# Zero products in TensorE's early waits and full-tile score biases for the first two head pairs, in a windowed-attention and gated token-mixing kernel on one core

## The chip, the core and the metric

The kernel runs on one core of a Trainium2 chip. The core has five engines that work side by side, each on its own list of instructions: TensorE (matrix products, written PE in the profile; PEld is its loading of weights), VectorE (DVE), ScalarE (ACT), GpSimd (POOL) and SyncE (SP). They wait for each other by semaphores. Products land in PSUM, everything else is in SBUF. The metric is the device time of one execution in microseconds; less is better. Three executions of the kernel before give a median of 172.1 us.

## What is computed

A windowed attention with a few global tokens, and a layer that mixes tokens and channels behind it. Inputs and output are float32; B = 4 batches, H = 8 heads, S = 768 tokens, D = 64, so d_model = 512; 8 global tokens, a window of 96.

```python
scores = scale * np.matmul(q, k.transpose(0, 1, 3, 2))
is_global = pos[None, :] < int(n_global)
is_local = (rel >= 0) & (rel < int(n_local))
dist = np.where(is_global & ~is_local, float(n_local), np.abs(rel))
scores = scores - slopes[:, None, None] * dist          # slope by head
scores = np.where(is_global | is_local, scores, -1e9)
a = softmax(scores);  x = (a @ v)  as [B, S, H * D]

theta = x @ w_theta
zr, zi = x * np.cos(theta), x * np.sin(theta)
y = einsum('ts,bsd->btd', w_tok_r, zr) + einsum('ts,bsd->btd', w_tok_i, zi)
u = x + y
out = u + np.maximum(u @ w_ch, 0.0)
```

## The kernel before

**Tiling.** Tokens lie in six tiles of 128. Heads go in four pairs p = 0 to 3, the two heads of a pair in the lower and upper 64 partitions of kT and qT (head dimension on the partitions, tokens along the row). Since a token sees at most the 95 before it and the 8 global ones, each key tile meets its own query tile and the next; kG holds the keys of a tile with those of the global tokens put in. The 11 blocks of a head are done in three chunks c = 0, 1, 2 (four, four and three blocks of 128 columns), so one chunk of a pair is a score tile pb of 128 x 2 x 512 in PSUM. Two such tiles exist (pool `big`); all smaller products take one of four rotating slots (pool `small`, tiles named ps).

**Batch 0** is written out by hand, in the order in which each engine runs it (lines 92 to 646): no scheduler moves anything there. Its exponentials are made by ScalarE from a score tile to which the bias has already been added in PSUM. For that `score_bias(p, c)` (L292) first writes `diag[h]` times `dist` into the tile, where `diag[h]` is the identity times -slope/scale and `dist` the table of distances (1e6 where nothing is seen); `score_mms` (L309, products at L325) then adds the keys times the queries on top, and `score_exp` (L331, L335) takes the exp. A score tile is free for the next bias when its exp has run.

`score_bias` has two forms. One makes two products of 128x128 weights, one for each head (L298). The other makes four of 64x64 weights (L305): since `diag` is diagonal, its two diagonal 64x64 quarters suffice, and for the second head of the pair rows and columns are swapped by halves, for which `distS` is `dist` with its halves of partitions swapped (`swap_distances`, L135, VectorE). Pair 0's chunks 0 and 1 take the first form, all others the second.

**The front of the program**, on TensorE: `warm(6)` makes six products of a tile of zeros into a slot of ps (L192, L195), the results of which nobody reads. Then come the biases of chunks (0,0) and (0,1), the transposes of pair 0's k and then q (`turn0`, L223, products at L221; they need the loaded and cast inputs), its scores for chunk 0 (`score_mms(0, 0, 0)`), which wait for the copies of the transposes to kT and qT (`out0`, L232) and to kG (`kglob`, L241 and L243) by ScalarE and VectorE. Then pair 1's transposes and the scores of chunk (0,1). The loop at L583 goes on over the pairs: exp of chunk (p,1), the copies of the next pair's kT, qT and kG, bias and scores of chunk (p,2), the products with the values of the pair before (`values`, L387), exp of (p,2), then bias, scores and exp of the next pair's chunk 0, bias and scores of its chunk 1, and the transposes of the pair after that. Behind it come theta (L428), the sines, the token mix (L453) and the channel product (L481), and the later batches, whose attention (with the bias as a factor after the exp) is woven between them.

## Time and profile before

| what | us |
|---|---|
| median of three runs | 172.1 (171.46, 172.1, 172.4) |
| the profiled execution, own time | 171.59 |
| its span, first to last instruction | 169.5 |
| TensorE busy | 157.9 (93% of the span) |
| VectorE busy | 126.7 (75%) |
| ScalarE busy | 104.6 (62%) |
| GpSimd busy | 38.9 (23%) |
| chain that ended last: TensorE's share | 62% |
| 64x64 bias products (L305), 40 of them, 394 to 400 ns each (median) | from 9.8 to 21.4 us |
| full bias products (L298), 4 of them, 634 ns each | from 3.7 to 5.0 us |
| products of the zero tile (L195), 6 of them, 634 ns each (median) | from 1.2 to 3.3 us |

Busy time counts a product from its start to its modelled end, and products overlap, so the duration of one is longer than the distance to the next. The span leaves out about 2.1 us around the first and last instruction. In the lists of instructions a row is: start, length, engine, line, operation, output <- inputs, shapes, and a count where equal instructions are merged; brackets hold the idle time before it on its engine and the instruction that ended this. In the chain of waits each row is one link, followed back from the end of the program.

### The profile page before, as it was taken

The numbers are of one execution on the slowest core, as the hardware profiler recorded it, in microseconds if no ns is written. First come the engines' busy times: TensorE is split into PE (matmuls) and PEld (weight loads), VectorE is DVE, ScalarE is ACT, GpSimd is POOL, SyncE is SP. The second block draws the span as 40 slices with busy tenths as digits, with TensorE's granted clock in tenths as the row PEclk, the third lists the DMA queues.
The fourth block names the chain that finished last, engine by engine and source line by source line (L and its number), as shares of the span: only waits on it lengthen the run. The fifth ranks groups of instructions, "written<-read, shape, count | busy, mean of one in ns | idle before, by whom it ended". The sixth has DMA issues, their size and how long they took to land.

```text
span 169.5 us, 3785 instructions
## 1 busy us (share of the span) xinstructions
PE 157.9 (93%) x1550; PEld 84.9 (50%) x1572; DVE 126.7 (75%) x265; ACT 104.6 (62%) x134; POOL 38.9 (23%) x46
## 2 busy tenths in 40 slices
PE   7579989999989999999989999999999999999991
PEld 2246665657655455545545464444555544444440
DVE  6848877699999997989998697787877837614442
ACT  4699898995599694799842641999257109400010
POOL 8975339005164101049700000000000000000000
PEclk9999999999999999999999999999999999999999
DMA  4999999999999999809999796777138472233335
GB/s 151 200 169 178 210 206 205 204 208 182 150 202 221 150 175 157 152 5 201 136 110 144 196 178 139 135 149 221 32 77 142 111 169 95 95 62 93 93 96 182
DMA packets 72704, 25.34 MB, mean 150 GB/s; under 512 B 60784, under 2 KB 69744, under 8 KB 72688
## 3 DMA queue, kind: packets, MB, share of 16 engines
q0 software_dynamic: 45696, 12.45, 88.6%
q1 hardware_dynamic: 26576, 12.13, 32.5%
q10 hardware_dynamic: 416, 0.52, 0.9%
q8 instruction: 12, 0.20, 0.6%
q14 instruction: 4, 0.03, 0.1%
HBM read 25.69 MB, written 6.29 MB: 189 GB/s over the span
## 4 chain that ended last, share of the span: by engine, by line
PE 62%; DVE 17%; ACT 13%; DMA 4%; issue 2%; DVEq 0%; SPq 0%
PE ps L453 27%; PE ps L481 9%; PE pb L428 6%; ACT e L335 5%; PE pb L325 5%; ACT cs L438 4%; PE pb L387 4%; PE ps L428 3%; DMA qk<-in_k_dram 3%; PE ps L267 2%; DVE x_sb L394 2%; DVE e L344 2%; DMA xT<-x_sb 2%; DVE kG L241 2%; PE ps L405 2%
## 5 line engine op out<-in xcount | busy, mean ns | idle before, releaser
L453 PE MATMUL ps<-zri,w_tokT 128*128 128x512 bf16 x272 | 67.8, 380 | 0.8 <-issue 0.2
L335 ACT ACTIVATE e<-pb 128x1024 bf16<-128x1024 f32 (+1 forms) x48 | 43.6, 955 | 16.7 <-PE pb L325 16.3
L453 PEld LDWEIGHTS <-w_tokT 128*128 128x128 bf16 x288 | 25.9, 98 | 27.3 <-DVE w_tokT L189 0.6
L458 DVE TENSOR_TENSOR u<-x_sb,ps 128x512 bf16<-128x512 bf16 x24 | 16.4, 684 | 13.3 <-PE ps L453 12.9
L481 PE MATMUL ps<-w_ch_bf,uT 128*128 128x512 bf16 (+1 forms) x96 | 23.9, 370 | 0.2
L442 DVE TENSOR_TENSOR zri<-x_sb,cs 128x1024 bf16<-128x1024 bf16 (+1 forms) x30 | 16.6, 581 | 5.0 <-ACT cs L438 4.7
L486 DVE SCALAR_TENSOR_TENSOR o_sb<-ps,u 128x512 f32<-128x512 f32 (+1 forms) x25 | 16.4, 664 | 4.4 <-PE ps L481 4.4
L325 PE MATMUL pb<-qT,kT 64*128 64x128 bf16 x224 | 15.4, 219 | 3.3 <-DVE qT L232 1.4
L344 DVE TENSOR_TENSOR e<-e,etab 128x1024 bf16<-128x1024 bf16 (+1 forms) x24 | 14.8, 620 | 2.3 <-ACT e L335 2.3
L325 PEld LDWEIGHTS <-kT 64*128 64x128 bf16 x224 | 8.8, 94 | 14.5 <-issue 10.5
L472 ACT COPY uT<-ps 128x512 bf16<-128x512 bf16 x7 | 4.2, 597 | 18.9 <-PE ps L471 18.8
L438 ACT ACTIVATE cs<-pb,halfpi 128x1024 bf16<-128x1024 f32 x8 | 8.9, 1115 | 10.7 <-PE pb L428 10.6
L428 PE MATMUL pb<-w_theta_bf,xT 128*128 128x512 bf16 x62 | 15.0, 379 | 0.2
L387 PEld LDWEIGHTS <-e 128*128 128x128 bf16 x352 | 12.7, 97 | 3.7 <-issue 1.2
L481 PEld LDWEIGHTS <-uT 128*128 128x128 bf16 x100 | 9.1, 98 | 9.9 <-ACT uT L472 0.8
L428 PEld LDWEIGHTS <-xT 128*128 128x128 bf16 x96 | 8.9, 98 | 10.1 <-DMA xT<-x_sb 0.6
L88 POOL DMA_DIRECT2D vn<-in_v_dram x5 | 9.6, 1916 | 11.4 <-DVE qkn L252 10.4
L325 PE MATMUL pb<-qT,kG 64*128 64x128 bf16 x128 | 11.8, 217 | 0.3 <-DVE kG L243 0.2
L394 DVE TENSOR_TENSOR x_sb<-pb,rec 128x768 bf16<-128x768 f32 x12 | 11.5, 958 | 0.4
L347 DVE TENSOR_TENSOR e<-e,etab 128x1024 bf16<-128x1024 bf16 x12 | 8.3, 689 | 2.9 <-ACT e L335 2.8
L387 PE MATMUL pb<-vn,e 128*128 128x65 bf16 x168 | 9.7, 193 | 0.3 <-DVE e L344 0.2
L273 ACT COPY kT<-ps 128x768 bf16<-128x768 bf16 x8 | 6.3, 800 | 5.2 <-PE ps L267 5.1
(81 smaller groups left out, 213.1 us busy)
## 6 DMA issues: line engine op xcount, KB each, us to landing
out_dram<-o_sb SPq DMA_DIRECT2D x23, 256.0 KB, 2.3
vn<-in_v_dram POOLq DMA_DIRECT2D x3, 768.0 KB, 23.1
qk<-in_q_dram POOLq DMA_DIRECT2D x2, 768.0 KB, 20.6
qk<-in_k_dram POOLq DMA_DIRECT2D x2, 768.0 KB, 22.2
w_nat<-in_moe_w_tok_r_dram POOLq DMA_DIRECT2D x3, 384.0 KB, 13.0
w_nat<-in_moe_w_tok_i_dram POOLq DMA_DIRECT2D x3, 384.0 KB, 14.1
vn<-in_v_dram POOLq DMA_DIRECT2D x2, 384.0 KB, 10.2
qk<-in_q_dram POOLq DMA_DIRECT2D x8, 96.0 KB, 10.1
```

The costliest lines, as they stand in the source:

```text
L325: nc.tensor.matmul(pb[:, hh, o:o + T], lhsT=lhsT, rhs=qT[R, (own, nxt)[part]], start=bool(b), stop=bool(b) or (jt == NT - 1 or (j == 1 and ...
L335: ins = nc.scalar.activation(e_c, pb[:, :, 0:n], AF.Exp, scale=scale).ins
L344: nc.vector.tensor_mul(e_c, e_c, tab[:, :, s0:s0 + n // T].rearrange("p a s n -> p a (s n)"))
L387: nc.tensor.matmul(po4[:, head - h0, it - i0], lhsT=l_, rhs=r_, start=(i_ == 0), stop=(i_ == len(mms) - 1))
L394: nc.vector.tensor_mul(xv, po4[:, :, :, 0:D], rec.to_broadcast([T, n, nt, D]))
L428: nc.tensor.matmul(pb[j_] if last else pb[:, j_, :], lhsT=xT[:, dc, st(j_)], rhs=w_theta_bf[:, dc, :], start=(dc == 0), stop=(dc == NC - 1))
L438: nc.scalar.activation(o, p_, AF.Sin, **bias)
L442: anchor["zri"] = nc.vector.tensor_mul(zri[b][:, i_, 2 * c + j_:2 * c + j_ + n, :].rearrange("p j (g d) -> p j g d", g=NP), xb[:, :, 2 * c ...
L453: anchor["pe"] = nc.tensor.matmul(ps, lhsT=w_tokT[wi][:, st, tt * T:(tt + 1) * T], rhs=zri[b][:, wi, st, :], start=(st == 0 and wi == 0), ...
L458: anchor["dve"] = nc.vector.tensor_add(u_sb[b, tt].rearrange("p (g d) -> p g d", g=NP), x_sb[b][:, :, tt, :], ps.rearrange("p (g d) -> p g ...
L481: nc.tensor.matmul(ps_c, lhsT=uT[:, dc, :], rhs=w_ch_bf[:, dc, i_ * n:(i_ + 1) * n], start=(dc == 0), stop=(dc == NC - 1))
L486: nc.vector.scalar_tensor_tensor(o_sb[:, cols], in0=ps_c, scalar=0.0, in1=u[:, cols], op0=ALU.max, op1=ALU.add)
```

## The change

Two things, in batch 0's hand-written part alone.

The full form of the bias is taken for all three chunks of pairs 0 and 1, so for (0,2), (1,0), (1,1) and (1,2) besides the two that had it. And `warm` is called three times more: with three products behind pair 0's second set of transposes, and with one product each before and after the bias of chunk (1,0).

```diff
         pb = pbs[0, p, c] = ps_big()
         n = min(4, 2 * NT - 1 - 4 * c)
         s0 = 2 if c else 0
-        if p == 0 and c < 2:
+        if p < 2:
             for hh in range(2):
                 nc.tensor.matmul(pb[:, hh, 0:n * T], lhsT=diag[:, 2 * p + hh],
                                  rhs=dist[:, s0:s0 + n].rearrange("p s n -> p (s n)"),
...
     turn0(0, 0)
+    warm(3)
     swap_distances()
     diagonals(1)
     out0(0, 1, act, 0)
...
         if p == 0:
             vglob(0, 0, 4)
+        if p == 0:
+            warm(1)
         score_bias(p + 1, 0)
+        if p == 0:
+            warm(1)
         score_mms(0, p + 1, 0)
         score_exp(0, p + 1, 0)
         score_bias(p + 1, 1)
```

## The prediction

> **What bounds the kernel now.** I read the page first: the span, the row of TensorE's busy tenths and the row of its granted clock.

> ```profile
> span 169.5 us, 3785 instructions
> ...
> PE   7579989999989999999989999999999999999991
> ...
> PEclk9999999999999999999999999999999999999999
> ```

> A slice is 4.24 us. From the fourth slice on TensorE is nearly always busy, so the tail is TensorE's, and what the front hands over late arrives late at the end. All edits lie in the first four slices. The PEclk row says full clock from the first slice. The durations by line say otherwise; the columns are the count and then minimum, median and maximum in ns, of products of one shape (128x512, bf16):

> ```profile
> L195 PE MATMUL ps<-zero x6: 608/634/634, 1.2 to 3.3; 128*128 128x512 bf16 x6
> ...
> L298 PE MATMUL pb<-dist,diag x4: 634/634/634, 3.7 to 5.0; 128*128 128x512 bf16 x4
> ...
> L453 PE MATMUL ps<-zri,w_tokT x272: 377/379/390, 31.4 to 162.4; 128*128 128x512 bf16 x136
> ```

> The same shape takes 634 ns up to 5.6 us and 379 ns later: TensorE starts slow, and the granted clock's row doesn't show it. When does it change? The transposes of L221 take 219 ns at 6.0 us and at 17.3 us alike, so in this execution TensorE is fast from 6.0 us on.

> Then TensorE's instructions in order of time: start, length, line, and in brackets the idle time before and what ended it.

> ```profile
> 3.73 1.91 PE L298 MATMUL pb<-dist,diag 128*128 128x512 bf16 x4
> 6.00 0.86 PE L221 MATMUL ps<-ident,qk 128*64 128x128 bf16 x24 [0.36 <-DVE qk L216]
> 8.31 0.34 PE L325 MATMUL pb<-qT,kT 64*128 64x128 bf16 x6 [1.44 <-DVE qT L232]
> ...
> 10.94 0.40 PE L305 MATMUL pb<-dist,diag 64*64 64x512 bf16 x2 [0.49 <-ACT e L335]
> ...
> 11.64 0.34 PE L325 MATMUL pb<-qT,kT 64*128 64x128 bf16 x6 [0.28 <-ACT kT L232]
> 12.18 0.23 PE L325 MATMUL pb<-qT,kG 64*128 64x128 bf16 x2 [0.20 <-DVE kG L243]
> ```

> Four waits: 1.44 us, ended by a VectorE copy of qT; 0.49 us, by the exp that frees a score tile; 0.28 us, by ScalarE's kT copy; 0.20 us, by VectorE's kG. Last the chain of waits (start, length, what), which says where TensorE itself is the limit:

> ```profile
> 8.31 0.40 PE pb L325 x8
> 8.71 0.79 PE ps L221 x24
> 9.50 0.35 PE pb L325 x8
> 9.87 1.02 ACT e L335
> ...
> 15.44 0.42 DVE kG L243
> ...
> 15.91 0.23 PE pb L325 x2
> 16.14 0.34 PE pb L305 x4
> 16.48 0.33 PE pb L325 x8
> ...
> 29.17 1.73 PE ps L428 x8
> ```

> From 8.31 to 9.87 us and from 15.91 to 17.6 us TensorE is on the chain. Between these the chain runs over ScalarE's exp and copies and VectorE's kG.

> **The change, part by part.** The instruction orders of VectorE, ScalarE, GpSimd and SyncE stay as they are, line for line, and no DMA moves. TensorE gets five products of the zero tile and loses eight: each of four bias chunks, (0,2), (1,0), (1,1), (1,2), is two full products instead of four of 64x64.

> *One product.* Eight 128x512 products in a row take 1.73 us (the last line above): 0.216 us each at the fast clock. The first six take 3.73 - 1.19 = 2.54 us: 0.42 us each at the slow one.

> *warm(3), after the second set of transposes.* These end issuing at 6.0 + 0.79 = 6.79 us; three products end by 7.44 us, at the slow clock by 8.06 us. The score products behind them wait for qT until 8.27 us. Cost 0; the cover is the wait of 1.44 us, and if that were gone the price would be 0.65 us.

> *A bias chunk.* From the four 64x64 products to the next line it is 0.34 us for 512 columns (15.14 to 15.48) and 0.29 us for 384 (9.82 to 10.11). Two full products stream for 2 x 0.216 = 0.43 us, or, at 384 columns, 0.32 us. So the lower bound is +0.09 and +0.03 us. Upper bound: the four 64x64 products run at once (their starts are 0.01 us apart), so 0.216 of the 0.34 us is one streaming pass, and 0.12 us goes into the turn to the next shape. If the full pair pays that as well: 0.55 and 0.45 us, so +0.21 and +0.16 us. I take the upper bound, since rows of 128x128 products that follow 64x128 ones (14.22 to 14.37 us) show a gap of that size. Two chunks of each length: +0.24 to +0.74 us of TensorE time.

> [...]

> *Where it lands*, with the upper bounds. Chunk (0,2) starts at 9.82 us when exp frees its tile; its scores end 0.16 us later, at 10.55 us, and their exp starts only at 11.5 us, behind a kT copy. The first warm(1) then fills 10.55 to 10.77 us, ahead of the exp that ends at 10.89 us: free. Chunk (1,0) 10.94 to 11.37, the second warm(1) to 11.59, the turn to 11.71 us, against 11.64 before: 0.07 us late for six products, but kG comes at 12.13 us and swallows it. Chunk (1,1): 12.35 us, 0.21 us late afterwards; its exp starts at 13.42 us, behind the exp before it, and its scores are there at 13.36 us: just free. The transposes behind it end at 14.09 instead of 13.88 us, and VectorE, busy until 14.07 us, loses about 0.03 us, which it has back before 15.09 us (it waits for kT there). Chunk (1,2) adds 0.16 us: 0.37 us late. The values products start at 14.74 us, the half-tile bias (2,0) at 15.51, its scores at 15.85, and the kG products at 16.05 us instead of 15.91. So 0.14 us come through to the chain; with the lower bounds (0.12 us late, against 0.26 us of room there) nothing does.

> *Slots.* The three calls of warm take three of the four rotating ps slots. The transposes at 13.02 us now reuse the slots of the pair before, whose copies end at 10.5 and 11.59 us: free. *distS* is written by 7.03 us and first read at 9.82 us, so to do without it earlier gains 0.

> *The sum* for an execution like the profiled one: 0 to +0.14 us on 171.59 us (span 169.5 us and 2.1 us around it), so 171.6 to 171.7 us.

> **What the zero products may bring.** The three runs lie from 171.46 to 172.4 us, 0.94 us apart, the profiled one near the lowest. Suppose TensorE becomes fast later in some executions. From 8.31 to 9.87 us the chain lies on TensorE for 0.40 + 0.79 + 0.35 = 1.54 us; with the slow durations (634 / 379 = 1.67) that is +1.03 us, about the spread. In 5.64 to 8.31 us TensorE is busy for only 0.86 us; warm(3) makes this 1.5 us, at the slow clock 2.1 us or more. The bounds of this are 0 (never late) and -1.03 us (late each time).

> [...]

> **Forecast and rivals.** About 0.5% is what a measurement of this kernel can tell from no change; here that is 171.24 and 172.96 us.

> *A, likeliest, 0.40:* the spread is a late clock in some executions, and it goes; all run like the profiled one: 171.7 us, own range 171.3 to 172.0. That is 0.2% under the median. For it: price and spread agree. Against: three runs are few.

> *B, 0.20, nothing:* the spread has another cause, TensorE is always fast by 6 us; 172.1 + 0.1 = 172.2 us. For it: the wait of 1.44 us did not make TensorE slow in the profile.

> *C, 0.25, faster:* the late clock is the usual case, and the profiled execution was not even free of other losses: 172.1 - 1.03 = 171.1 us. For it: TensorE is busy in only 0.82 of the 1.8 us from 10.4 to 12.2 us, where the clock could go as well. Against: the profiled execution is fast there and takes 171.59 us.

> *D, 0.15, slower:* the clock is late, and the zero products do not release it; then they run at 0.42 us between 10.9 and 12.2 us. Chunk (1,0) and the second warm(1) last until 10.94 + 3 x 0.42 = 12.2 us, six scores at the slow clock follow to 12.55 us, 0.4 us behind kG's arrival, and the slow full chunks (1,1) and (1,2) add 0.28 and 0.16 us (0.85 against 0.34 x 1.67 = 0.57; 0.64 against 0.48). With the 0.14 us: 172.1 + 1.0 = 173.1 us. It decides from the point where TensorE is still slow at 10.9 us. Against: in the profile it is fast 4.9 us before that.

> That the change does not do what it says (zero products that miss the waits) has no place of its own: they need no data but the tile written at 0.86 us, and stand between the transposes and the waiting scores.

> **How the numbers follow.** The time is A's, 171.7 us. The range takes in A and B and most of C: 171.0 to 172.6 us. Faster is C, 0.25; same is A and B, 0.60; slower is D, 0.15.

> **What would show it.** After: L195 x11, three of them near 6.85 us with 380 ns or 634 ns (which tells the clock at once); the L325 products still at 8.31 us, released by qT; kG still released by VectorE at 12.18 us; L325 on kG at 15.9 to 16.05 us; full pairs followed by the next line after 0.43 to 0.55 us; runs closer together than 0.9 us. I am wrong if TensorE's products after 6 us are slow in either trace, if the pairs take over 0.6 us, or if the stages behind 24 us differ by more than the front does.

## The result, and the profile after

| | before | after |
|---|---|---|
| first comparison, 22 executions each: median (lowest to highest), us | 172.51 (171.46 to 173.95) | 171.62 (171.13 to 172.33) |
| its ratio, 95% interval | | 0.995 [0.9931, 0.9968] |
| second comparison, 35 and 12 | 171.98 | 171.85, ratio 0.9999 [0.997, 1.0027] |
| third comparison, 29 and 12 | 172.29 | 171.64, ratio 0.9981 [0.9954, 1.0008] |
| profiled execution: own time, span | 171.59, 169.5 | 171.37, 169.3 |

The ratios leave out executions more than 1.5% above the fastest of their kernel, which here are executions of before alone, so means over all executions are given as well.

The predicted 171.7 us stands beside 171.62. The two profiled executions differ by 0.2 us only, so the gain cannot be read from this pair. First, what the edits did where they stand: TensorE after the change, in order of time (start, length, line; in brackets the idle time before and what ended it).

```profile
6.01 0.86 PE L221 MATMUL ps<-ident,qk 128*64 128x128 bf16 x24 [0.66 <-DVE qk L216]
6.80 0.82 PE L195 MATMUL ps<-zero 128*128 128x512 bf16 x3
8.31 0.34 PE L325 MATMUL pb<-qT,kT 64*128 64x128 bf16 x6 [0.69 <-DVE qT L232]
...
9.82 0.48 PE L298 MATMUL pb<-dist,diag 128*128 128x384 bf16 x2
10.24 0.23 PE L325 MATMUL pb<-qT,kT 64*128 64x128 bf16 x2
...
12.18 0.23 PE L325 MATMUL pb<-qT,kG 64*128 64x128 bf16 x2
12.35 0.59 PE L298 MATMUL pb<-dist,diag 128*128 128x512 bf16 x2
12.88 0.23 PE L325 MATMUL pb<-qT,kT 64*128 64x128 bf16 x2
...
15.99 0.22 PE L325 MATMUL pb<-qT,kG 64*128 64x128 bf16 x2
16.14 0.40 PE L305 MATMUL pb<-dist,diag 64*64 64x512 bf16 x2
```

The scores start at 8.31 us as before; the three zero products have halved the wait ahead of them, from 1.44 to 0.69 us. (The first of the two single zero products has no row in this trace, but the loads of their weights number 11, as they should.) A full pair takes 0.53 us until the next line at 512 columns (12.35 to 12.88) and 0.42 us at 384 (9.82 to 10.24). The kG products of pair 2 start at 15.99 us instead of 15.91. The chain of waits shows how far this carries. Before (start, length, what):

```profile
12.45 1.94 ACT e L335 x2
14.38 0.70 ACT kT L232
...
15.11 0.31 DVE kG L241
...
17.65 0.96 DVE qT L232
```

After:

```profile
12.41 0.54 PE pb L298 x2
12.95 0.33 PE pb L325 x8
13.28 0.79 PE ps L221 x24
14.07 0.43 PE pb L298 x2
14.50 0.27 PE pb L325 x6
14.77 0.77 PE ps L387 x22
15.54 0.34 PE pb L305 x4
15.88 0.33 PE pb L325 x8
...
17.71 0.96 DVE qT L232
```

Where the chain ran over exp and copies from 12.45 to 15.86 us, it now runs over TensorE without a break, and VectorE gets pair 3's q at 17.71 us instead of 17.65, 0.06 us late. By the first sine, some 9 us later, this lateness is gone (first row before, second after):

```profile
26.97 1.11 ACT L438 ACTIVATE cs<-pb,halfpi 128x1024 bf16<-128x1024 f32 x1 [0.41 <-PE pb L428]
26.89 1.11 ACT L438 ACTIVATE cs<-pb,halfpi 128x1024 bf16<-128x1024 f32 x1 [0.43 <-PE pb L428]
```

So in an execution like the first one profiled the edits cost 0.06 us at 17.7 us and nothing that can be seen at the first sine, which moves by more than that from one execution to the next (e1 below). The gain must come from executions that were not like it.

### The profile page after: what moved, and what is told of

The parts are those of the page before. It is cut to its first block, busy times and chain, and to the rows that moved or that the text cites. A ratio compares the mean times of both kernels' runs of the same rounds, so it can differ in the third digit from the quotient of the medians.

```text
span 169.3 us, 3778 instructions
## 1 busy us (share of the span) xinstructions
PE 158.8 (94%) x1546; PEld 85.1 (50%) x1569; DVE 126.7 (75%) x265; ACT 104.6 (62%) x134; POOL 38.8 (23%) x46
## 3 DMA queue, kind: packets, MB, share of 16 engines
q0 software_dynamic: 45696, 12.45, 87.8%
q1 hardware_dynamic: 26576, 12.13, 32.5%
## 4 chain that ended last, share of the span: by engine, by line
PE 64%; DVE 16%; ACT 11%; DMA 4%; issue 2%; DVEq 0%; SPq 0%
PE ps L453 27%; PE ps L481 9%; PE pb L428 6%; PE pb L325 5%; ACT cs L438 4%; ACT e L335 4%; PE pb L387 4%; PE ps L428 3%; DMA qk<-in_k_dram 3%; PE ps L267 2%; DVE x_sb L394 2%; DVE e L344 2%; DMA xT<-x_sb 2%; PE ps L405 2%; DVE e L347 2%
## 5 line engine op out<-in xcount | busy, mean ns | idle before, releaser
L453 PE MATMUL ps<-zri,w_tokT 128*128 128x512 bf16 x272 | 67.8, 380 | 0.8 <-issue 0.2
L335 ACT ACTIVATE e<-pb 128x1024 bf16<-128x1024 f32 (+1 forms) x48 | 43.6, 955 | 16.6 <-PE pb L325 16.1
L453 PEld LDWEIGHTS <-w_tokT 128*128 128x128 bf16 x288 | 25.8, 98 | 27.3 <-DVE w_tokT L189 0.6
L325 PE MATMUL pb<-qT,kT 64*128 64x128 bf16 x224 | 15.4, 219 | 2.2 <-DVE x_sb L394 0.9
L325 PEld LDWEIGHTS <-kT 64*128 64x128 bf16 x224 | 8.8, 94 | 14.4 <-issue 10.3
L428 PE MATMUL pb<-w_theta_bf,xT 128*128 128x512 bf16 x62 | 15.0, 379 | 0.2
L428 PEld LDWEIGHTS <-xT 128*128 128x128 bf16 x96 | 8.9, 98 | 10.0 <-DMA xT<-x_sb 0.6
L325 PE MATMUL pb<-qT,kG 64*128 64x128 bf16 x128 | 11.8, 216 | 0.1
L394 DVE TENSOR_TENSOR x_sb<-pb,rec 128x768 bf16<-128x768 f32 x12 | 11.5, 958 | 0.4
## 6 DMA issues: line engine op xcount, KB each, us to landing
vn<-in_v_dram POOLq DMA_DIRECT2D x2, 384.0 KB, 10.4
```

Of the source, the lines that this page charges most:

```text
L325: nc.tensor.matmul(pb[:, hh, o:o + T], lhsT=lhsT, rhs=qT[R, (own, nxt)[part]], start=bool(b), stop=bool(b) or (jt == NT - 1 or (j == 1 and ...
L335: ins = nc.scalar.activation(e_c, pb[:, :, 0:n], AF.Exp, scale=scale).ins
L394: nc.vector.tensor_mul(xv, po4[:, :, :, 0:D], rec.to_broadcast([T, n, nt, D]))
L428: nc.tensor.matmul(pb[j_] if last else pb[:, j_, :], lhsT=xT[:, dc, st(j_)], rhs=w_theta_bf[:, dc, :], start=(dc == 0), stop=(dc == NC - 1))
L453: anchor["pe"] = nc.tensor.matmul(ps, lhsT=w_tokT[wi][:, st, tt * T:(tt + 1) * T], rhs=zri[b][:, wi, st, :], start=(st == 0 and wi == 0), ...
```

## The experiments

Each timed kernel has 12 executions, with the mean granted clock of each. "Lost" counts those under 0.9945: one stretch of 3.41 us at half clock (8.72 to 12.14 us in e1) takes 0.010 off the mean over 170 us, and a fall in the last microseconds, when TensorE has little left to do, 0.002 in the changed kernel's profile and 0.005 in e5's. All executions with a known clock, over four chips for before (the 22 executions of before in the first comparison, mean 172.53 us, have none on record and are left out):

| kernel | executions | mean us | lost | of these 0.980 and under (by this sum two such stretches or more) |
|---|---|---|---|---|
| before | 110 | 172.12 | 46 | 21 |
| changed kernel (first, e5, e10) | 46 | 171.71 | 0 | 0 |
| five zero products alone (e2) | 12 | 171.84 | 0 | 0 |
| warm(3) alone (e4, e11) | 24 | 171.81 | 1 | 0 |
| three quarter-array products (e7) | 12 | 171.64 | 0 | 0 |
| one zero product (e6) | 12 | 171.72 | 3 | 0 |
| two ahead of the transposes (e9) | 12 | 171.80 | 1 | 0 |
| full-tile biases alone (e3, e8) | 24 | 171.89 | 9 | 0 |
| the two single products alone (e12) | 12 | 172.08 | 8 | 2 |

**e1: the kernel before, once more.** No edit.

> The kernel before, unchanged, seen in one more execution. Theory 1 (late clock): the 22 times of before lie mostly near 172.5 us, 0.9 us above the execution that was profiled, so this execution should show TensorE slow past 6.0 us: products of L221 or L325 at 6.0 to 10 us longer than 219 ns, the exp of chunk (0,1) starting 0.3 to 1.0 us later than 9.87 us, and a time of about 172.5 us. If it is fast from 6.0 us on, its time should be under 172.0 us. Theory 2 (the spread of before has nothing to do with the front): a time near 172.5 us with the same durations and starts up to 17 us as in the first profile.

171.91 us, mean clock 0.988: the time is not the 172.5 us that theory 1 had put for a slow execution. By stretches (start:end, length, busy us of PE, PEld, DVE, ACT and POOL with counts, then granted clock, DMA share, GB/s):

```profile
6.00:7.00 1.00, 0.86 (x24) 0.70 (x24) 0.95 (x3) 0.43 (x2) 1.00 (x2) 1.00 1.11 154
7.00:8.00 1.00, 0.00 (x0) 0.09 (x1) 0.99 (x5) 0.97 (x5) 1.00 (x2) 1.00 1.27 189
8.00:9.00 1.00, 0.70 (x17) 0.60 (x17) 0.79 (x5) 0.80 (x3) 1.00 (x2) 0.86 1.52 180
9.00:10.00 1.00, 1.00 (x22) 0.83 (x18) 0.00 (x0) 0.76 (x1) 1.00 (x3) 0.50 2.24 160
10.00:11.00 1.00, 1.00 (x14) 0.47 (x12) 0.90 (x1) 0.36 (x1) 1.00 (x3) 0.50 2.43 157
11.00:12.00 1.00, 0.79 (x14) 0.49 (x10) 0.06 (x1) 1.00 (x2) 0.46 (x1) 0.50 1.76 182
12.00:13.00 1.00, 0.70 (x12) 0.22 (x8) 0.47 (x2) 1.00 (x2) 0.00 (x0) 0.93 1.35 193
```

The clock does not come late: TensorE is fast at 6 us, does nothing from 7 to 8 us, and is at half clock from 8.7 to 12.1 us. The trace's record of the clock has the changes at 5.31, 8.72 and 12.14 us, about 3.41 us apart each time. On the chain of waits the second pair's transposes, 0.79 us before, then take this:

```profile
8.30 0.40 PE pb L325 x8
8.70 1.37 PE ps L221 x24
10.06 0.56 PE pb L325 x8
...
10.64 1.02 ACT e L335
```

The exp of chunk (0,1) starts at 10.64 us instead of 9.87: 0.77 us late. The first sine starts at 27.45 us instead of 26.97, so some 0.48 us of that arrives behind batch 0; in traces that kept the clock the first sine also starts at 26.88 (e2), 26.89 (the changed kernel) and 27.06 us (e4), so this figure from one pair is rough. Theory 1 stands in a changed form, the clock is lost and not late.

**e2 to e4: the parts of the change, each alone.**

In e2, the five zero products with the bias chunks as before:

```diff
     turn0(0, 0)
+    warm(3)
     swap_distances()
...
+        if p == 0:
+            warm(1)
         score_bias(p + 1, 0)
+        if p == 0:
+            warm(1)
         score_mms(0, p + 1, 0)
```

In e3, the full-tile biases without zero products:

```diff
-        if p == 0 and c < 2:
+        if p < 2:
             for hh in range(2):
```

In e4, only the first three zero products:

```diff
     turn0(0, 0)
+    warm(3)
     swap_distances()
```

> The five zero products alone; the bias chunks stay in 64x64 form. Theory 1a (the zero products release the clock): the whole gain, 0.995 of before, or 0.07 us better than the changed kernel, since chunk biases cost 0.07 us less: 0.9945 to 0.996. Theory 1b (the gain comes from the full-tile biases, which use the whole array): 0.999 to 1.001. Theory 2 (neither; it is in the slots or in chance): no forecast between them.

> The full-tile biases alone, without the five zero products. Theory 1a: no gain, and the 0.07 us by which the second pair's scores come late on the chain: 1.000 to 1.001. Theory 1b (they keep TensorE fast): 0.995 to 0.997.

> The three zero products behind the transposes alone. Theory 1a in its narrow form (the 1.44 us wait decides when TensorE becomes fast): the whole gain, 0.9945 to 0.996. If the clock is lost only later, in the sparse stretch from 10.4 to 12.2 us: 0.999 to 1.001 here, and the gain comes back only with the two single products. Theory 1b: 0.999 to 1.001.

Ratios to before: 0.9993 [0.997, 1.0016], 0.9992 [0.9967, 1.0018], 0.9989 [0.9961, 1.0017]. None of them tells the theories apart, and none reached the 0.995 that the first comparison had led me to expect. The clocks do: with zero products 0 of 24 executions lost it, with the full-tile biases alone 6 of 12. The profiled execution of e3 is one of these:

```profile
7.00:8.00 1.00, 0.00 (x0) 0.09 (x1) 0.99 (x5) 0.97 (x5) 1.00 (x2) 0.91 1.28 191
8.00:9.00 1.00, 0.70 (x12) 0.50 (x13) 0.79 (x5) 0.59 (x3) 1.00 (x2) 0.50 1.57 182
```

Here it goes at 7.8 us, 3.41 us after TensorE became fast. So in these runs the three products behind the transposes, which e2 and e4 share, were enough. The profiled execution of e2 kept its clock and still took 172.38 us. TensorE became fast only at 7.15 us (the first set of transposes takes 1.39 us instead of 0.86, the scores start at 8.56 us instead of 8.31), but by the first sine, at 26.88 us against 26.97 before, nothing of that is left. What it did lose is among its waits from 59 to 73 us (who waited for whom, us in total, times, longest):

```profile
PE pb L428 <- DMA xT<-x_sb: 1.0, 1, 1.0
```

A DMA transpose of x, issued while the next batches are being loaded, landed late (on the chain from 58.52 us for 9.99 us); in the changed kernel's profile, and in the first one of before, there is no such wait in that stretch. So there is at least one other cause of spread, worth about 1 us in this trace, that shows far behind the front. How often it strikes is not known; with a spread of that size 12 executions do not show 0.2% in a median.

**e5 to e8: again, how many products, and what counts.**

e5 is the changed kernel and e8 is e3, both without a further edit. e6, against before:

```diff
     turn0(0, 0)
+    warm(1)
     swap_distances()
```

e7, against before:

```diff
+    def warm_q(n):
+        ps = ps_small([T, 512], FP)
+        for _ in range(n):
+            nc.tensor.matmul(ps[0:64], lhsT=zero[0:64, 0:64], rhs=zero[0:64], start=True, stop=True)
...
     turn0(0, 0)
+    warm_q(3)
     swap_distances()
```

> The changed kernel again, beside others on one chip. In the look at the kernel before TensorE was fast at 6.0 us and half as fast from 8.7 to 12.1 us: a stretch of 3.41 us at half clock lowers the mean granted clock by 0.010. Theory 1 (the change keeps that stretch from happening): no execution with a mean clock under 0.9945, as in all 22 of it so far, while 14 of 29 of before had one; the ratio is 0.995 to 0.999 (half of the executions times 0.5 to 1 us, less 0.07 us). Theory 3 (the 0.995 was largely the chip or the hour): 0.999 to 1.001.

> One zero product behind the transposes instead of three, nothing else. Windows of 3.41 us that begin when TensorE becomes fast held 1.50 and 1.54 us of TensorE work where the clock fell, 1.7 us and more where it stayed. If about half a window of work is what counts, one product (0.22 us) brings those two windows to 1.72 and 1.76 us: between none and 15% of the executions under 0.9945 (before: 48%), ratio 0.997 to 0.999. If three are needed, 30 to 50% of them, ratio 0.9985 to 1.0005.

> Three zero products of 64x64 weights, a quarter of the array, in the place of the three full ones; nothing else. They take the same time each. If the clock goes by how long TensorE is busy: no execution under 0.9945, like the full three (0 of 12). If it goes by how much of the array works: 1.54 us and a quarter of 0.65 us are 1.70 us, at the edge, so 10 to 40% of the executions under 0.9945.

> The full-tile biases alone, once more, for more executions. Theory 4 (they end a slow stretch after one window, because full products keep the array busier in it): again about half of the executions at 0.985 to 0.991, and none at 0.980 or under, where before had 6 of 29. If that was chance: one or more in five of the executions at 0.980 or under. Ratio 0.998 to 1.000 by theory 4, 1.000 to 1.001 otherwise.

Ratios: 0.9999 [0.997, 1.0027], 0.9995 [0.9969, 1.0022], 0.9986 [0.9955, 1.0017], 0.9993 [0.9967, 1.0019]. Lost: 0, 3, 0 and 3 of 12. e5's ratio alone would speak for theory 3, that the first 0.995 was the chip or the hour; its clocks speak for theory 1, and e10 below has a ratio in theory 1's range. One product was too little for all cases (3 of 12, more than the 15% that I had put as the bound), three lost none in e5 (0 of 12), nor did three of 64x64 weights in e7 (0 of 12), which speaks for TensorE's busy time and against the share of the array (more on this below). e8 again has no execution at 0.980 or under; with e3 that is none of 24, where before has 21 of 110, and 10 of the 64 on the same two chips.

For each profiled execution I then took the window of 3.41 us that begins when TensorE becomes fast. The first busy number is TensorE's. Lost, in e1, e3, e12 and e6:

```profile
5.31:8.72 3.41, 1.51 (x37) 1.11 (x38) 3.35 (x12) 2.53 (x8) 3.41 (x5) 1.00 1.24 175
```

```profile
4.42:7.83 3.41, 1.54 (x27) 0.89 (x26) 2.82 (x8) 2.15 (x7) 3.41 (x4) 1.00 1.22 190
```

```profile
5.66:9.07 3.41, 1.63 (x48) 1.45 (x50) 3.07 (x12) 2.53 (x8) 3.41 (x5) 1.00 1.40 186
```

```profile
5.00:8.41 3.41, 1.68 (x31) 0.99 (x31) 3.35 (x11) 2.66 (x8) 3.41 (x4) 1.00 1.27 184
```

Kept, in before's first profile, in the changed kernel and in e11 (the three products alone):

```profile
5.81:9.22 3.41, 1.77 (x52) 1.60 (x54) 2.92 (x12) 2.56 (x8) 3.41 (x4) 1.00 1.33 174
```

```profile
4.92:8.33 3.41, 2.07 (x31) 1.02 (x31) 3.23 (x10) 2.65 (x7) 3.41 (x4) 1.00 1.27 184
```

```profile
5.66:9.07 3.41, 2.38 (x51) 1.66 (x53) 3.07 (x12) 2.54 (x8) 3.41 (x5) 1.00 1.31 176
```

In these traces the border lies between 1.68 us (e6) and 1.77 us (before), 0.49 and 0.52 of 3.41. It is the same kernel that loses the clock with a window from 5.31 us and keeps it with one from 5.81: half a microsecond later, the window takes in more of what follows the wait. With the three products the window from 4.92 us holds 2.07 us. The later windows of the same grid fit: in the profiles of before and of the changed kernel those after which the clock stayed held 2.4 us or more, and in the changed kernel's it falls at 168.76 us, after a window with 0.20 us; in e3 the window up to 168.26 us held some 2.1 us, and its mean clock of 0.990 leaves no room for a second fall. The closest pair is e12 and e11: both windows begin at 5.66 us, the only difference inside them is the three products, and 1.63 us lost the clock where 2.38 us kept it.

The mean clocks say the same of executions without a trace. In the nine traces in which such a last fall comes before the span ends, it comes 163.84 us (48 windows) after TensorE first became fast (4.92 and 168.76 us in the changed kernel). So span and mean clock together give an estimate of when TensorE became fast, within 0.2 us in those traces (4.8 for 4.92 us in the changed kernel, 4.3 for 4.35 in e5, 5.4 for 5.31 in e1). Of before's kept executions 15 have a mean clock from 0.995 to 0.999: nine became fast at 4.3 us or earlier by this estimate, six at 5.6 us or later, none between. Of the 20 with 0.985 to 0.989, which lost one window, 17 became fast between 4.4 and 5.5 us by the same sum. The changed kernel has 13 executions between 4.3 and 5.5 us, and all kept the clock.

The same estimate bears on e7. Five of its executions became fast at 4.7 to 4.95 us; without the zero products such windows hold 1.3 to 1.4 us (from 4.70 us in e9 and 4.92 us in the changed kernel, less the zero products' time), and a quarter of the 0.76 us that e7's three add would bring them to 1.6 us at most, where the clock was lost. They kept it.

**e9 to e11: another place, and the size.**

e10 is the changed kernel and e11 is e4, without a further edit. e9, against before:

```diff
     cast0(1, act, 1)
+    warm(2)
     turn0(0, 1)
```

> Two zero products ahead of the transposes, in the short wait for the casts (0.36 to 0.9 us), instead of three in the long wait behind them; nothing else. If the clock goes by the work in a window of 3.41 us, and not by that one long wait, the windows that held 1.5 to 1.7 us of work hold 1.9 us and more: at most 1 of 12 executions under 0.9945. Where TensorE is still slow at 5.6 us the two products last until 6.5 us and the transposes start 0.5 us late, so the mean time is 171.7 to 172.1 us in spite of it. If filling the long wait is what counts: a third to a half of the executions under 0.9945 and a mean of 172.0 to 172.4 us.

> The changed kernel a third time, for the size. By the clock alone: before loses it in 26 of 64 executions, which are 0.85 us slower in the mean than its others (172.07 us over all, 171.67 us where it keeps it), so the ratio of the means is 0.998, and the ratio here 0.9965 to 0.9995; no execution under 0.9945. If the first comparison's 0.995 is the size: 0.993 to 0.997.

> The three zero products behind the transposes alone, again. If they are all that the change gives, its mean is that of the changed kernel beside it within 0.2 us, or up to 0.1 us better, as the bias chunks stay shorter; no execution under 0.9945. If the full-tile biases or the two single products add something, it is 0.2 us or more behind.

Ratios: 0.9984 [0.9954, 1.0013], 0.9981 [0.9954, 1.0008], 0.9981 [0.9953, 1.0009]. Lost: 1, 0 and 1. Two products in another wait of the same window did nearly as well as three in the long one. In e9's profiled execution the long wait is still 1.43 us, and the clock stays, with a window of 1.83 us:

```profile
4.70:8.11 3.41, 1.83 (x29) 1.02 (x28) 2.99 (x8) 2.45 (x7) 3.41 (x4) 1.00 1.25 178
```

So in these runs the loss went with the window's sum, and not with the one wait. e11's one loss contradicts "none"; no trace of it is at hand. warm(3) alone (171.81 us, 24 executions) and the whole change (171.71, 46) differ by 0.1 us with standard errors of 0.08 and 0.06: not told apart. No version was clearly better than the changed kernel.

**e12: the single products alone.**

```diff
         if p == 0:
+            warm(1)
         score_bias(p + 1, 0)
         if p == 0:
+            warm(1)
```

> The two single zero products around the bias of chunk (1,0) alone. They lie behind the first window, so theory 1 lets the clock fall as often as before: 3 to 7 of 12 executions under 0.9945. Of 93 executions of before 19 had two slow windows or more (0.980 and under), of 24 with the full-tile biases alone none. If what ends the slow stretch is TensorE's work in the slow window, to which both edits add, it ends after one window here as well: none at 0.980 or under, and a mean of 171.8 to 172.1 us. If it is the full-tile biases themselves, 1 to 4 of 12 at 0.980 or under and a mean of 172.0 to 172.4 us.

Ratio 1.0021 [0.9995, 1.0046], mean 172.08 us (before beside it 172.05); 8 of 12 lost, 2 of them at 0.980. So the singles alone gain nothing and, by these two mean clocks, do not always end the slow stretch after one window. That fits the case of the full-tile biases themselves, but 2 of 8 lost executions against none of 9 with full tiles is too few to show it.

How full tiles could shorten the stretch is open. The slow windows that ended after 3.41 us held 2.94 to 3.30 us of TensorE work. No execution with two of them behind the first wait was profiled, but e2's start shows the other side. TensorE became fast at 7.15 us there; counted back by 3.41 us at a time, the window from 0.33 to 3.74 us, with 2.55 us of work, left it slow, and the next one, with 3.04 us, ended that. (The granted clock reads 1.00 here all the same; that TensorE is slow shows in L298's products of 634 ns.)

```profile
0.33:3.74 3.41, 2.55 (x7) 0.75 (x7) 2.58 (x14) 1.36 (x2) 2.85 (x9) 1.00 0.43 131
3.74:7.15 3.41, 3.04 (x27) 1.58 (x28) 2.05 (x6) 1.83 (x4) 3.41 (x4) 1.00 1.20 233
```

So in these traces it took more work to get the clock back (2.55 us were too little in e2) than to keep it (1.77 us were enough in before).

## Why the prediction was right, and where not

*The time and the sign.* 171.7 us and "within 0.5%" hold. Over all executions with a known clock the means are 172.12 (before, standard error 0.07) and 171.71 us (0.06): a ratio of 0.9976 [0.9965, 0.9986]. On the two chips where both kernels ran with known clocks (64 and 24 executions) they are 172.13 and 171.74 us. The first comparison's 0.995 was the largest of three, and the others' intervals reach 1; its 22 executions of before had a median of 172.51 us where the later ones have 172.1.

*Case A's outcome is what happened.* The 64 executions of before that keep the clock have a mean of 171.66 us, the changed kernel 171.71: all its executions run like the good ones, to within the errors of 0.06 us each. None of its 46 lost the clock. That 171.7 us came out so closely is in part luck: the figure was read off one profile, and that execution happened to be one that kept its clock.

*Case A's mechanism was wrong in its first half.* I put a late clock ahead of the wait. The clock was there in time and was lost in or after the wait of 1.44 us, since the window around that held too little work (1.51 us in e1). In B I had counted it as evidence that this wait "did not make TensorE slow in the profile"; that one execution had been on the good side of the border by less than 0.1 us. The sign that I had set for being wrong, slow products after 6 us in either trace, did not show in the two profiled executions; it took e1 to see it. A late clock exists too (e2), but in that trace it had cost nothing by the first sine, and the zero products came only behind it there (7.15 and 7.33 us).

*The price was mis-sized.* I had 1.03 us for each late execution. Executions with one slow stretch are 0.71 us slower in the mean than those with none (25 executions at 172.37 us), with more than one 1.57 us (21 at 173.23). Over all 110 that is 0.46 us, before's distance from its own kept executions, and the changed kernel gained 0.41 us of it. I also took the spread of 0.94 us for the clock alone, so that price and spread agreed was chance: the executions that keep the clock still lie from 171.0 to 172.7 us, for which a late DMA like e2's (1.0 us there) may be one cause. "Runs closer together than 0.9 us" fails for the same reason; the first 22 of the changed kernel lie 1.2 us apart.

*The bias chunk.* I took the upper bound, 0.55 and 0.45 us; measured 0.53 and 0.42. The kG products were put at 16.05 us and came at 15.99, 0.08 us late where 0.14 were forecast; 0.06 us reached VectorE at 17.71 us, and nothing that can be seen at the first sine. By the 0.216 us of a product in L428's row of eight, 0.43 of the pair's 0.53 us is the two products themselves, which is an estimate; the four 64x64 products took 0.34 us before (15.14 to 15.48 us). What I had not counted is that full tiles may shorten a slow stretch: alone they have a mean of 171.89 us against 172.07 in the 64 executions of before beside them, with standard errors of 0.09 each, which is not clear of noise.

*The rivals.* B (nothing, since the spread has another cause) is out for the time, as the ratio of the means lies clear of 1; another cause there is as well, e2's late DMA. C (faster by over 0.5%) needed the clock lost in most executions; it is 42%. The sparse stretch from 10.4 to 12.2 us that C named did not lose it in before's first profile: the window from 9.22 to 12.64 us around it held 2.44 us and the clock stayed. D (a slow clock that the zero products don't release) did not occur. Nothing in the traces after waits for distS or for a slot of ps, as worked out.

## What to carry to other kernels

One profile of a kernel whose times spread is one draw: before costing a wait as free, look at the mean clock of several executions, and profile more than one. Count TensorE's work in the first stretch after it has become fast, for every place where that stretch may begin: in the traces here the clock was lost where the first 3.41 us held 1.68 us or less, and stayed with 1.77 us or more. In the worse draws the lost clock cost more than the length of the wait of 1.44 us: by their mean clocks the executions with more than one slow stretch were 1.57 us behind those with none. A few products of a zero tile in that wait cost nothing here (the scores still start at 8.31 us) and took the bad draws away (46 of 110 executions of before lost the clock, none of 46 of the changed kernel). Whether the full-tile biases add to that is not shown: the three products alone are at 171.81 us, the whole change at 171.71.
